# Conformer block: rows of whole chunks transposed by DMA instead of TensorE, with a new plan

## The chip, the cores and the metric

The kernel runs on one core of one Trainium2 chip. The core has five engines, each with its own in-order queue: TensorE (PE, matrix products and transposes into PSUM), VectorE (DVE), ScalarE (ACT), GpSimd (POOL) and SyncE (SP, which here only issues transfers). The metric is the device time of one execution, the median of several runs.

## The reference

One conformer block over x of shape (2, 4000, 144) in bfloat16: a half feed-forward, attention with 4 heads of 36, a gated depthwise convolution of 5 taps, a second half feed-forward, a last norm.

```python
h = _layernorm(x); h = _silu(h @ w_ff1a) @ w_ff1b; x = x + 0.5 * h
h = _layernorm(x); qkv = h @ w_qkv            # q, k, v: (B, 4, 4000, 36)
p = _softmax(einsum('bhqd,bhkd->bhqk', q, k) * 36 ** -0.5)
x = x + einsum('bhqk,bhkd->bhqd', p, v) @ w_o
h = _layernorm(x) @ w_pw1; a, b = h[..., :144], h[..., 144:]
h = a * _sigmoid(b); c = sum(pad(h)[:, i:i+4000, :] * dw[i] for i in range(5))
x = x + _silu(c) @ w_pw2
h = _layernorm(x); x = x + 0.5 * (_silu(h @ w_ff2a) @ w_ff2b)
return _layernorm(x)
```

## The kernel before, in words

**Tiling.** The 8000 tokens are 16 chunks of 500, 8 for each batch entry. A chunk is four blocks of 125 tokens; a block has its tokens on partitions in X and XN. Products need the features on partitions, 72 at a time in two halves, so every normalised row (here a "row" is one chunk's layer norm output or attention output) is turned over: into XT for the products of a feed-forward, of the attention's output and of the gate, into XTQ for queries, keys and values. That is five rows a chunk, 80 in all: the first feed-forward, queries/keys/values, attention output, gate, second feed-forward.

**How a row is turned.** `ln` (L888) takes the statistics on DVE and normalises block by block into XN, on POOL in the middle of the program, on DVE with POOL's power function in the front and the tail. `transp` (L877) then takes one PSUM bank, issues eight PE transposes (four blocks by two halves) and one copy out of PSUM, on DVE or, where ACT has less to do, on ACT (`flex`, L823). `parts` (L947) cuts a chunk into two half rows in the front (until the keys of the first batch entry, chunks 0 to 7, are done) and in the tail. Then a half row takes one bank, four transposes and one smaller copy. Chunk 0 goes by `pre_first` (L1139), the others by `ff1` and `pre2` (L1132, L1173), `post1` (attention output and gate, L1273) and `post2` (convolution and second feed-forward, L1398).

**Attention.** For each chunk of queries (a phase; the first two chunks have two phases each, L1515) the keys come in 62 tiles of 64 and a last one of 32. `emit_S` (L1541) computes the scores of a tile, four heads in two PSUM banks; `emit_exp` (L1555) has ACT take the exponential of both banks at once (128x1000) into a slot of PT; `emit_O` (L1623) multiplies PT with the values VA on PE. `dve_tile` (L1569) does a tile's exponential on DVE instead, in five steps: two int16 results from the score banks, taken one at a time, a mask (uint16), a product, a second mask. It yields two factors in two slots of PT, both of which are multiplied with the values. `due` (L1795) decides which tiles go there.

**Order.** A planner, which runs while the program is built, simulates the engines with costs written in the code and emits the operations in the order that it finds; POLICY holds its settings for 49 segments. `reorder` (L249) then shifts each engine's steps by the letters of ORDER (P is no shift; a letter for each step, trailing P's left off), and `place` (L227) gives each PSUM tile the bank that PLACES names, one digit for each tile in the order in which the tiles are taken. A pair of banks for ACT's exponential has one digit. So the order on every engine is fixed before the run, and an operation whose input is late stops its engine. Stores and loads are issued by SP, a few by ACT.

**Memory.** QT holds the queries of all 16 chunks. While the first two chunks' first phases wait for their second, their sums lie in SAVE, a part of QT not yet filled (L1466); `epilogue` (L1476) copies each chunk's result over queries that are used up.

Of the kernel before, what the change touches and what calls it, by code (L numbers as in the profile page):

```python
# [12 lines left out]
D = 144  # L13
# [23 lines left out]
        "PPPPPPPPPPPPQQRROKPPPPQQNQOQOPQOPPPPQOPRPNQOeOxRMMzPRKLHMNROMKMEOQLJOOQOIQKNQKMOOKOMOMNOOQNQQLQTNOYN"  # L37
        "NOSQTQKKTPQRSQWQ^BRW`EPWQ[GQ[EQ]RY]S?BBRWSZU?CCFUGQVTHKKNQSPPXPHQQNLOSNPQMPPPPPPQOPRRRMMPPPTPNPNQOSO"
        "PQMPPQOPPPPPPQOPQOQSNPRPLQOPPPPPPPPPPPPPPPPPPPPPPPPPPQOPPPPPQOPPQOPQOPPPPPPPPQOPPQOPPPQQNPPQOPPPRPRP"
        "RROIQOSQSQLLQOSOPNQQNSOOUPTLPVQUJQIWQKSQIMMTPPPLTPPROQSQHRMOQOPROOPPQOROOQQNPROOQQNQOPPTOOOOPPPPPPQQ"  # L40
        "NPPPPQQNPPQOPQQNPQOPPPQOPQOPQOQOPPPPPPPPPPPPPQOPQOPPPPPPPPPPPPPPPPPPPQSNPQRLOPPPPPPPPQOPQQNPPPPPQOPP"
        "PQQNPPPQTNOOQNPPPPPPPPPPPPPQRPMQOPPQOPPTOOPNQQNPROOSSNNNUPNSNOMQQQRLUNOOOOROOPROOPPPPQOPSPNQNQQQMPPS"
        "OOQNPPPRPNQOUPNOPNPPROOQQNQQQMPRPNQRNQNPQORPQMQOPQQNQOPPPQOPPPPPPPPPQOPQOPQQNPPPPPPPPPPQOPPPTOOOOSOP"
        "RPSKOOQTNOORNTPMORRMRRRKRLRRRLRRKRRRKSQKRRLTPLTOMRNQMQQSMSNROLQQSMOOQQNQQNQSNPRRLNROOQQNPQOQQQMSPNQQ"
        "MQQQRLQQQLQSNROULPNRNNQQQMROOQQQMRPNQQNQQNQQQMQRNQQRLQRMQQRLRPSLPRMSPMQRMSPMQRRLQRLQQMQRRTLPLTNOPRMQ"
        "QQTKPNQQTLPNQQRLQNQQRRRKTTKNNQMRPNPPPPQOQQNQOPROQNQOPQOQOQOPQQNPPPPPPPPPPPPPPPPPPPPPPPPPPROOPPPPQOPP"
        "PPPPROOPSOPNPPPPPPROOPPPPPPPPPPPPPPPPPPQOPPPPPPQOPQOPPQQNPPPPPPPPPQOPPPPPPPPPPPPPPPPQOPPSPNRPRPQQIPP"
        "WOOOOQRMQRKOQOQWNOQNNRNNROQNQOPQQNPPPQOPPPPQOPPPROOPPPPPPPPPPPQOPPPPPPPPPPPPPQOPPPPPQOPPPQQNPPPPPPPP"
        "PPPROOPPRPNPPPPPPPPPPPPPTOQNNPPPQOPQOTUPMMNOQQSMOQNQTNOORNQSMOQSMSOMQQMRROMQSSSSKMKQQNPRPNROOPPPPQQN"
        "PQQNPQOPSPNOPPSOOOPPPPROOPPQOPPPPPPPPPPPPPPPPPPPPRSQSLLOPPQOPQOPQQNPPQOQOQOQOPPQOQOPQOPQOPPPPPPPPPPP"  # L50
        "QOPQOPPPPPPPQOPPPQOPPPPPQOPPPQOQOSQNQQLPPPPPPPPRORNOPPPPPPPQOPPPQOQQQQLROOQOQQQMQOQQQMQQQMQOQQQQLPPP"
        "PPPPPPPPPPPPPPQOPPQOQOPRPNPPPPPQRNVNOQNNQNRPNQQSMOQNRPQMRPNSOOQNQOPPPSOOTNOOOPQOQQQQLPQOQQNROOQQNQOQ"
        "QQQQKQQQMPPRPQQQKQQNROQNPPPPPPPPPPPQQNQOPPPQQNSPNOPPSPRRLMPQOPPQOPQOPPPQOQOROOSOOSNOQNQOQQQMPPROOPPP"
        "PPQQNPPSOOOPPPPPPPPPPSOOOPPPROOQQRMQNPQOPPPPQQNPPPPPPPPPPPPQOPPQOPPSOOOPQOTQNNOPQOPPQOQQNPPPPPUPNYNY"
        "MMNVNUOPSHIIPQOPPPQQNPQOPPUOQNNQQQLPPPPPPPPPPPQQSPLOQOPRPNPQOTOPNOQOPPROQRMOPQOSOPQMROOQQNPPPRPNPQOP"
        "PPPPPPPPPPPPPPPPPPPPPPPQQNPPQOPPPPQOPPPPPPPPPPPPPPPPTPPPQQQITUSMMMMQOQOQQNRRSSLLNQOPROOPPPPQOROOPPQQ"
        "QQQKPPQQQQLPPPPPPPPPPPPPPPPPPPPPPPPPPPPPPPPPPQQNSQNTRLNQMPPQOPPQOQOPPPPSSPSQKKQOQQQMQQQMQQQMQRNOQOPQ"
        "RNOSPNQQQLQQQMQOQQNPQQNPPPQQQQLRVNNOOOOPRSNNQQMQQQMTOOOOPPPPSQNNQOPPQOPRPNPPTRNNNPRPNQOPPQOPPSOOOPPP"
        "PPPPPQOPQOPQQNPSSNNNPQQNPQRNQQMQOQQNROOPPQQQQLPQSNOQNQRNOSORNNQOPQOQOPQOPPQRPMQTTMNNNSOOQNPPQOQOPPPQ"
        "OPROOPQOPPPPPPPPPPPPPPPPPPPPSOPNQOPPRPNQOPPQOPQQNQQNRPNPQQNQOQQQMROOQOPRRSMRLRMQQMQOSPPRLOPQOPQQNPPP"  # L60
        "QOPPPPPPPPPPPPPPPPPRRNNPPPPRPNRPRMRNOPPQQNROOPQQNPPPPPPPPRPNQQNROOPQSNOQNPRRNSPLQNPQOPPQOPPQOPPPQOQQ"
        "NPPPQQNPPPPPPPPPPQOPPPPPPPPPPPPPPQOPQOQOQOQOPPPPPPPPQOPPPPPPQOQOQOPPQOROOQQQQLQQNQRRMQMROOPQQNQRPMQO"
        "ZQOXLNNWMPXKKOUIOLNNQSNPNQQNROOPVOOOOOOQOROQQMQRPMQOPPQOPPPPPQOPPPPPPQOPPPPQOPQOSOPQMROOPPPPQOPPPPPP"
        "PPPPPPPPUOQNNRSMNSNROMPPQOPPPPPPPPPPPQOPQOQOQOPPQOQRRMRMOQRRRLTPKRNNQQQMPSOOOPQQNPSOOOPPPQOPPRPNVPUM"
        "QSLRRRIRRGNPQOZOPX_WKLPKKKKQQQSPGUIOOPNPQOROOPPPQOPSQOMPPPPPPPPPPPPROOPPPROOPQOPPPPQO"
    ),
    "act": (
        "PPPPPPPPPPPPROOPQQNPPPPPPPPPPPPPQRSMNOPPPQOQQNQOQQSMPSMOOPPQOQOPPPPPPPPPPPPPPPPPPQRNOPROOPPPPPPPPPQO"
        "PPPPPPPPPPPPPPPPPPPPPPPPPPPPPPPPPPPPPPPPPPPPPPPPPPPPPPPPQOQQNQQNPPPPQOPPPPPPPPPPPPPPPPPPQOPPPPPPPPPP"
        "PPPPPPPPPPPPPPPPPPPPPPPPPPPPPPPPPPPPPPPPPPQOPPPPPPPQOPPQOPPPPPPPPPPPPPQQNPQOPPPPPPPPPPPPPPPPPPPPPPPP"  # L70
        "PPPPPPPPPPQQNPPPPPPPPPPPPPPPPPPPPPPPPPPPPPPPPPPPPPPPPPPQOPPROOPPPPPROOQOPPPPPPPPPPPPPPPPPPPPPPPPPPPP"
        "PPPPPPPPPPPPPPPPPPPPPPPPPPPPPPPPPPPPQOPPPPPPPPPPPPPPPPPPPPPPPPPPPPPPPPPPPPPPPPPPPPPPPROOPPQRNOPPPPPP"
        "PPPPPPPPPPPPPPPPPPPPPPPPPPPPPPPPPPPPPPPPPPPPPPPPPPQOPPPPQOPPPPQOPPPPPPPPPPPPPPPQOPPPPPPPPPPPPPPPPPPP"
        "PPPQOPPPPPQOPPPQOPPQOPPPPPPPPPPPPPPPPPPPPPPPPPPPPPPPPPPPPPPPPQOPPPPPPPPPPPPPPPQOPPPROOROOPPPQOPPPPPP"
        "PPPPPPPPPPPPPPPPPPPPPPPPPPPPPPPPPPPPPPPPPPQQNPPPPPPPPPPQOPPPPPPPPPPPPPPPPPPPPPPPPPPPPQOPPPQOPPPPPPPP"
        "QOPPPPPPPPPPPPPPPPPPPPPROOPPPPPPPPPPPPPPPPPPPPPPPPPPPPPPPPPPPPPPPPQOPPPPPPQOPPPPPPPPPPPPPPPPPPPPPPPP"
        "PQOPQOPPPPPPPPPPQOPPPPPPPPPPPPPPPPPPPPPPPPPPPPPPPPPPPPPPPPPPPPPPPPPPPQOPQOPPQOPPQOPPPQOPPPQOPPPPPPPP"
        "PPPPPPPPPPPPPPPPPPPPPPQOPPPPPPPPPPPPPQOPQOPPPPPPPPPPPPPPPPSSNNNQQNROOPPPPPQQNPPPQRPQQQQIPQOPPQO"
    ),
# [1812 lines left out]
```

## Time and profile before

| | us |
|---|---|
| median of 3 runs | 905.8 (905.73 to 905.96) |
| span of the profiled execution | 903.7 |
| first / last exponential on ACT starts | 19.7 / 869.5 |
| exponentials on ACT, on DVE | 841, 167 |
| TensorE's granted clock, mean | 0.997 |

Line 353 is the helper that records every operation, so groups are told apart by the tiles that they write and read (out<-in). "DVE COPY XT<-PS" is the copy after a row's transposes, "PE MATMUL PS<-IDENT,XN" the transposes themselves, "PT<-PS" the exponentials. Behind a group stand its busy time, the mean of one in ns, and the engine's idle time ahead of it with the releaser.

### The profile page before, as it was taken

What the parts mean: (1) busy time and instruction counts of PE and PEld (TensorE: products, weight loads), DVE (VectorE), ACT (ScalarE), POOL (GpSimd) and SP (SyncE); (2) the same over time, 40 slices, a digit from 0 to 9 for tenths busy, and PEclk for the clock granted to TensorE, in tenths of its full rate; (3) what the DMA queues carried; (4) which work ended last, traced back from release to release, by engine and by line L of the source; (5) the groups of instructions that cost most, each with busy time, mean ns of one, the idle gap of its engine ahead of it and who ended that gap; (6) DMA issues with size and microseconds to landing.
All of it is one profiled execution on the core that took longest, in us unless ns stands there. A gap on an engine that the chain in (4) does not pass through costs nothing.

```text
span 903.7 us, 27474 instructions
## 1 busy us (share of the span) xinstructions
PE 878.2 (97%) x11946; PEld 409.1 (45%) x11946; DVE 808.1 (89%) x1756; ACT 869.2 (96%) x1105; POOL 278.5 (31%) x519
## 2 busy tenths in 40 slices
PE   8999999999999999999999999999999999999996
PEld 6644434454443443444444444444434444434366
DVE  8988888889999998999988799897899799978987
ACT  6899999999999999999999999999999999999984
POOL 5121213136211702421404441270215460323143
PEclk9999999999999999999999999999999999999998
DMA  4000000000000000000000000000000000000000
GB/s 123 27 2 2 1 2 1 2 3 1 2 3 1 3 2 3 1 3 1 2 2 1 15 2 2 15 8 1 1 3 8 14 9 2 3 1 10 6 8 27
DMA packets 7322, 7.36 MB, mean 8 GB/s; under 512 B 2376, under 2 KB 7202, under 8 KB 7202
## 3 DMA queue, kind: packets, MB, share of 16 engines
q1 hardware_dynamic: 5786, 5.00, 1.8%
q8 instruction: 93, 1.52, 0.7%
q10 hardware_dynamic: 1416, 0.62, 0.3%
q14 instruction: 27, 0.22, 0.1%
HBM read 3.31 MB, written 2.30 MB: 6 GB/s over the span
## 4 chain that ended last, share of the span: by engine, by line
ACT 48%; PE 42%; DVE 6%; POOL 2%; issue 1%; DMA 0%; POOLq 0%; DVEq 0%
ACT PT L353 43%; PE PS L353 42%; ACT TH L353 5%; DVE PT L353 3%; POOL RS L353 1%; POOL XN L353 1%; DVE ST L353 1%; DVE HT L353 1%; DMA X<-in_x_dram 0%; DVE QT L353 0%; DVE XN L353 0%; DVE XT L353 0%; DVE KT L353 0%; DVE X L353 0%; DVE RS L353 0%
## 5 line engine op out<-in xcount | busy, mean ns | idle before, releaser
L353 ACT ACTIVATE PT<-PS 128x1000 bf16<-128x1000 f32 (+1 forms) x841 | 777.7, 1063 | 5.9 <-PE PS L353 4.0
L353 PE MATMUL PS<-QT,KT 64*64 64x500 bf16 x3968 | 416.1, 385 | 10.7 <-ACT PT L353 6.0
L353 PE MATMUL PS<-PT,VA 64*37 64x500 bf16 x4636 | 394.6, 373 | 2.1 <-DVE PT L353 0.9
L353 DVE TENSOR_SCALAR PT<-PS 128x500 int16<-128x500 f32 x334 | 222.1, 670 | 21.0 <-PE PS L353 18.5
L353 PEld LDWEIGHTS PS<-QT,KT 64*64 64x64 bf16 x3968 | 122.2, 104 | 216.1 <-ACT PT L353 122.3
L353 POOL TENSOR_SCALAR RS<-ST 125x4 f32<-125x4 f32 x112 | 34.0, 304 | 475.2 <-DVE ST L353 469.5
L353 PEld LDWEIGHTS PS<-PT,VA 64*37 64x37 bf16 x4636 | 131.9, 96 | 95.9 <-DVE PT L353 22.0
L353 DVE TENSOR_SCALAR PT<-PT 128x1000 uint16<-128x1000 uint16 x334 | 137.7, 421 | 2.6
L353 POOL TENSOR_SCALAR XN<-X,RS 125x144 bf16<-125x144 bf16 x224 | 132.4, 605 | 8.0 <-DMA out_dram<-XN 2.3
L353 POOL TENSOR_TENSOR RS<-RS,NHALF 125x4 f32<-125x4 f32 (+1 forms) x101 | 95.3, 948 | 94.7 <-DVE RS L353 89.9
L353 DVE TENSOR_TENSOR PT<-PT 128x1000 bf16<-128x1000 bf16 x167 | 113.5, 682 | 1.6
L353 ACT ACTIVATE TH<-PS 128x500 bf16<-128x500 f32 (+3 forms) x198 | 107.0, 563 | 3.3 <-PE PS L353 2.1
L353 DVE SCALAR_TENSOR_TENSOR HT<-TH,PS 128x500 bf16<-128x500 bf16 (+1 forms) x135 | 81.1, 616 | 18.8 <-ACT TH L353 18.4
L353 PE MATMUL PS<-XT,WA 72*128 72x500 bf16 (+2 forms) x280 | 71.6, 359 | 0.5 <-DVE XT L353 0.3
L353 DVE SCALAR_TENSOR_TENSOR X<-PS,X 125x288 bf16<-125x288 f32 x128 | 57.2, 451 | 12.4 <-PE PS L353 10.9
L353 DVE BATCH_NORM_STATS2 ST<-X 125x6 f32<-125x288 bf16 (+1 forms) x160 | 66.1, 447 | 1.2 <-DMA X<-in_x_dram 0.8
L353 PE MATMUL PS<-WB,HT 128*125 128x144 bf16 (+1 forms) x640 | 52.4, 230 | 0.0
L353 PEld LDWEIGHTS PS<-WB,HT 128*125 128x125 bf16 (+1 forms) x640 | 44.3, 136 | 13.0 <-issue 5.1
L353 PE MATMUL PS<-IDENT,XN 125*72 125x125 bf16 x512 | 42.9, 221 | 3.1 <-POOL XN L353 1.7
L353 DVE COPY XT<-PS 72x1000 bf16<-72x1000 bf16 (+2 forms) x65 | 40.1, 617 | 4.7 <-PE PS L353 4.2
L353 PEld LDWEIGHTS PS<-IDENT,XN 125*72 125x72 bf16 x512 | 31.8, 112 | 23.4 <-issue 11.4
L353 PEld LDWEIGHTS PS<-XT,WA 72*128 72x128 bf16 x280 | 20.3, 97 | 30.4 <-issue 7.1
(86 smaller groups left out, 573.3 us busy)
## 6 DMA issues: line engine op xcount, KB each, us to landing
X<-in_x_dram SPq DMA_DIRECT2D x16, 140.6 KB
out_dram<-XN SPq DMA_DIRECT2D x14, 140.6 KB
WA<-in_w_ff1a_dram ACTq DMA_DIRECT2D x1, 144.0 KB
WB<-in_w_ff1b_dram ACTq DMA_DIRECT2D x1, 144.0 KB, 2.8
WA<-in_w_ff2a_dram SPq DMA_DIRECT2D x1, 144.0 KB
WB<-in_w_ff2b_dram SPq DMA_DIRECT2D x1, 144.0 KB
out_dram<-XN SPq DMA_DIRECT2D x2, 70.3 KB
WQKV<-in_w_qkv_dram ACTq DMA_DIRECT2D x1, 121.5 KB
```

What stands on the lines that cost most here:

```text
L353: ins = getattr(eng, o.name)(*o.a, **o.k)
```

## The change

- XN, AN and XT get blocks of 128 columns for each half of 72 (`[NB, 2, 128]`), so that a row is 128 x 1024; XT's buffer XTB can be read as before or as DMA leaves it, with a block every 256 columns. The columns between are cleared once for each buffer by POOL, ten clearings. A stored row uses XN densely, as XNC.
- `small(c)` says where half rows remain: in the tail, and in the front for chunks 0 to 3 alone (FULL = 4). Before, the whole front had them. Chunks 4 to 7 are therefore normalised as whole rows on POOL.
- A whole row is turned by one `dma_start_transpose` from SP. For queries, keys and values the result goes to an XT buffer, and two more transfers copy it into XTQ. There is no PSUM bank, no PE transpose and no copy by DVE or ACT for such a row.
- QT shrinks to a ring of NQR = 12 chunks. The queries of chunks 12 to 15 wait until the attention of chunks 1 to 4 has left its slot. SAVE moves to the second batch entry's keys.
- POLICY, ORDER and PLACES are new throughout. Their lengths:

| table | before | after |
|---|---|---|
| PLACES, digits | 1778 | 1735 |
| ORDER pe, act, dve, pool, sp, letters | 2885, 1095, 1613, 127, 13 | 2885, 1075, 1646, 135, 94 |

```diff
+    NQR = 12
+    NLANE = 12
+    FULL = 4
+    LAT_C = 2.2
+    SP_T = 1.2
+    LAT_T = 2.5
-    XN = sb("XN", [NXN, NB, D])
+    XN = sb("XN", [NXN, NB, 2, 128])
-    XT = sb("XT", [NXT, 2, CW])
+    XTB = sb("XTB", [NXT, 2 * NB * 128])
-    QT = sb("QT", [2, N])
+    QT = sb("QT", [2, NQR * CH])
-    AN = sb("AN", [NAN, NB, D])
+    AN = sb("AN", [NAN, NB, 2, 128])
...
+    XT = XTB[:, :, 0:2 * CW].rearrange("p s (k n) -> p s k n", k=2)
+    XTD = XTB[:, :, :].rearrange("p s (i k n) -> p s i k n", i=NB, k=2)
+    def xt(s, k, i0, i1):
+        if s in by_dma:
+            return XTD[0:HD, s, i0:i1, k, 0:TB]
+        return XT[0:HD, s, k, i0 * TB:i1 * TB].rearrange("p (i n) -> p i n", i=i1 - i0)
...
+    def small(c):
+        return mode["tail"] or mode["front"] and c < FULL
...
+    def dma_transp(src, rk, s, wk):
+        j = lanes[0] % NLANE
+        lanes[0] += 1
+        yield need("sp")
+        by_dma.add(s)
+        op("sp", "dma_start_transpose", XTB[:, s, :].rearrange("p (j n) -> p j n", n=128),
+           src.rearrange("p i k n -> p (i k n)"), q=f"t{j}", r=[rk], w=wk + [("LANE", j)], cost=SP_T, lat=LAT_T)
...
-        calm = mode["front"] or mode["tail"]
+        calm = small(c)
+        if n == NB and not calm and not store and ("XN", u) not in clear:
+            clear.add(("XN", u))
+            yield need("pool")
+            op("pool", "memset", XN[:, u, :, :, :], 0.0, w=[("XN", u)], cost=0.8)
...
     def ln_tr(c, s, bs, e=False):
         u = yield from ln(c, bs, e)
         rows, c0 = TB + e, bs[0] * TB
+        if len(bs) == NB and not small(c):
+            yield from dma_transp(XN[:, u, :, :, :], ("XN", u), s, [("XT", s, i) for i in bs])
+            xnp.give(u)
+            return
...
     def ln_trq(c, bs):
...
+        if len(bs) == NB and not small(c):
+            s = yield need("sp", xtp)
+            yield from dma_transp(XN[:, u, :, :, :], ("XN", u), s, [("XT", s, i) for i in bs])
+            xnp.give(u)
+            yield need("sp")
+            for k in range(2):
+                j = lanes[0] % NLANE
+                lanes[0] += 1
+                op("sp", "dma_start", XTQ[0:HD, k, c0:c0 + CH].rearrange("p (i n) -> p i n", i=NB),
+                   XTD[0:HD, s, :, k, 0:TB], q=f"t{j}", r=[("XT", s, i) for i in bs],
+                   w=[("XTQ", c % CPB, i) for i in bs] + [("LANE", j)], cost=0.6, lat=LAT_C)
+            xtp.give(s)
+            return
...
-    def parts():
-        return [range(0, 2), range(2, 4)] if mode["front"] or mode["tail"] else [range(0, 4)]
+    def parts(c):
+        return [range(0, 2), range(2, 4)] if small(c) else [range(0, 4)]
...
+        wrap = nm == "WQ" and c >= NQR
+        bk = yield need("pe", banks, dur=0.42, cond=(lambda: not saved) if over or late else (
+            lambda: c - NQR + 1 in otf_done) if wrap else None)
...
         def part(bs):
-            yield from transp(AN[0:TB, a, bs[0]:bs[-1] + 1, :], ("AN", a),
-                              XT[0:HD, s1, :, bs[0] * TB:(bs[-1] + 1) * TB], [("XT", s1, i) for i in bs], len(bs))
+            if len(bs) == NB and not small(c):
+                yield from dma_transp(AN[:, a, :, :, :], ("AN", a), s1, [("XT", s1, i) for i in bs])
+            else:
+                by_dma.discard(s1)
...
-    SAVE = QT[:, 1, T:T + 4 * CH * NQ].bitcast(F32).rearrange("p (c k n) -> p c k n", c=NQ, k=2)
+    SAVE = KT[:, 1, 1, 0:4 * CH * NQ].bitcast(F32).rearrange("p (c k n) -> p c k n", c=NQ, k=2)
```

The products read XT through `xt` and `xt1` (one block), and `blocks` gives their PSUM side the same shape. `lat` is what the planner takes for the time from the end of an operation to its result.

More of the change, by code (lines that the diff above doesn't have):

```diff
@@ L126 @@
+    '36321430641340365200542643146141321'
 )
@@ L227, in place @@
     def place(self, slot, n):
-        no, at = len(self.tiles), int(PLACES[len(self.tiles)])
+        no, at = len(self.tiles), slot if PLACES is None else int(PLACES[len(self.tiles)])
         self.tiles.append(tuple(range(at, at + n)))
@@ L809, in setup_qk @@
                    cost=0.3)
+    clear = set()
     def now(k):
@@ L881, in transp @@
             for i in range(n):
-                op("pe", "transpose", ps[:, k, i, 0:rows], src[:, i, k * HD:(k + 1) * HD], IDENT[0:rows, 0:rows],
+                op("pe", "transpose", ps[:, k, i, 0:rows], src[:, i, k, 0:HD], IDENT[0:rows, 0:rows],
                    r=[rk, "ID"], w=[("ps", bk)], cost=0.055, kind="f")
@@ L886, in transp, with halves, ln @@
         banks.give(bk)
-    def ln(c, bs, e=False):
+    def halves(ap):
+        return ap.rearrange("p (k d) -> p k d", k=2)
+    def ln(c, bs, e=False, store=False):
         n, b0, rows = len(bs), bs[0], TB + e
+        xn = (lambda u, j: XNC[0:rows, u, j, :]) if store else (lambda u, j: XN[0:rows, u, j, :, 0:HD])
+        xi = (lambda j: X[0:rows, c * NB + b0 + j, :]) if store else (lambda j: halves(X[0:rows, c * NB + b0 + j, :]))
         xe = ["XE"] * e
@@ L916, in ln @@
             for j in range(n):
-                op("act", "activation", XN[0:rows, u, j, :], X[0:rows, c * NB + b0 + j, :], ACT.Identity,
+                op("act", "activation", xn(u, j), xi(j), ACT.Identity,
                    bias=RS[0:rows, u, 2, j:j + 1], scale=RS[0:rows, u, 0, j:j + 1],
@@ L935, in ln_tr @@
         rows, c0 = TB + e, bs[0] * TB
-        yield from transp(XN[0:rows, u, 0:len(bs), :], ("XN", u), XT[0:HD, s, :, c0:c0 + len(bs) * rows],
+        if len(bs) == NB and not small(c):
+            yield from dma_transp(XN[:, u, :, :, :], ("XN", u), s, [("XT", s, i) for i in bs])
+            xnp.give(u)
+            return
+        by_dma.discard(s)
+        yield from transp(XN[0:rows, u, 0:len(bs), :, :], ("XN", u), XT[0:HD, s, :, c0:c0 + len(bs) * rows],
                           [("XT", s, i) for i in bs], len(bs), rows)
@@ L968, in mm2 @@
         for k in range(2):
-            op("pe", "matmul", PSV[0:rows, bk, 0:CH], lhsT=W0[0:HD, k, m0:m1], rhs=XT[0:HD, s, k, 0:CH], start=k == 0,
+            op("pe", "matmul", blocks(PSV[0:rows, bk, 0:CH]), lhsT=W0[0:HD, k, m0:m1], rhs=xt(s, k, 0, NB), start=k == 0,
                stop=k == 1, r=[("XT", s, i) for i in range(NB)] + wk, w=[("ps", bk)], cost=c_pe(CH), kind="f")
@@ L988, in ff_tile @@
                 for g in (1, 0):
-                    op("pe", "matmul", PSV[:, bk, 0:2 * TB], lhsT=WE[0:HD, k, 64 - 64 * g:192 - 64 * g],
-                       rhs=XT[0:HD, s, k, g * 2 * TB:(g + 1) * 2 * TB], start=k == 0 and g == 1, stop=k == 1 and g == 0,
+                    op("pe", "matmul", blocks(PSV[:, bk, 0:2 * TB]), lhsT=WE[0:HD, k, 64 - 64 * g:192 - 64 * g],
+                       rhs=xt(s, k, 2 * g, 2 * g + 2), start=k == 0 and g == 1, stop=k == 1 and g == 0,
                        r=[("XT", s, 2 * g), ("XT", s, 2 * g + 1)] + [(nm, "a", j) for j in (1, 2, 3)],
@@ L1067, in proj @@
         cc = c % CPB
-        over = nm == "WQ" and p == 1 and c >= CPB
-        late = nm == "WQ" and p == 0 and c >= NCH - 4
-        bk = yield need("pe", banks, dur=0.42, cond=(lambda: not saved) if over or late else None)
+        over = nm == "WK" and p == 1 and c >= CPB
+        late = nm == "WQ" and p == 0 and NQR - 4 <= c < NQR
+        wrap = nm == "WQ" and c >= NQR
+        bk = yield need("pe", banks, dur=0.42, cond=(lambda: not saved) if over or late else (
+            lambda: c - NQR + 1 in otf_done) if wrap else None)
         for k in range(2):
@@ L1076, in proj @@
         copy(dst, PSV[:, bk, 0:CH], [("ps", bk)], [(nm + "T", c)] + [("SAVE", i) for i in range(NQ) if over]
-             + ["OTF0"] * late, CH, scale=Q_SCALE if nm == "WQ" else 1.0)
+             + ["OTF0"] * late + [("WQT", c - NQR), ("OT", c - NQR), ("OT", c - NQR + 1)] * wrap, CH, scale=Q_SCALE if nm == "WQ" else 1.0)
         if nm == "WK" and cc == CPB - 1:
@@ L1133, in ff1 @@
         s = yield need("dve", xtp)
-        kids = S.spawn(ln_tr(c, s, bs) for bs in parts())
+        kids = S.spawn(ln_tr(c, s, bs) for bs in parts(c))
         yield need("pe", kids=kids)
@@ L1176, in pre2 @@
         yield need("dve")
-        kids = S.spawn(ln_trq(c, bs) for bs in parts())
+        kids = S.spawn(ln_trq(c, bs) for bs in parts(c))
         yield need("pe", kids=kids)
@@ L1292, in after @@
             yield from gen
-        kids = S.spawn(part(bs) for bs in parts())
+        kids = S.spawn(part(bs) for bs in parts(c))
         if c == NCH - 1:
@@ L1495, in epilogue @@
         else:
-            op("dve", "tensor_copy", OTF[:, :, :], ps, r=rk, w=["OTF", "OREL"], cost=c_dve(2 * CH))
+            op("dve", "tensor_copy", OTF[:, :, :], ps, r=rk, w=["OTF", "OREL"] + k0, cost=c_dve(2 * CH))
+        otf_done.add(c)
         a = yield need("dve", anp)
+        if ("AN", a) not in clear:
+            clear.add(("AN", a))
+            yield need("pool")
+            op("pool", "memset", AN[:, a, :, :, :], 0.0, w=[("AN", a)], cost=0.8)
         for zz in range(2):
@@ L1859, in bass_standalone__conformer_family_zipformer__speech_kernel @@
     R.stats = stats
-    R.reorder(ORDER)
+    if ORDER is not None:
+        R.reorder(ORDER)
     R.finish(group_qs=("w0", "w1", "w2", "w3"))
```

204 lines of the change are left out of this document (107 added, 97 removed), and 92 rows, old and new, of the table POLICY.

## The prediction

> **What bounds the kernel now.** I read the busy shares first, then the same by stages, then the groups of instructions, then the chain of waits.
>
> ```profile
> span 903.7 us, 27474 instructions
> PE 878.2 (97%) x11946; PEld 409.1 (45%) x11946; DVE 808.1 (89%) x1756; ACT 869.2 (96%) x1105; POOL 278.5 (31%) x519
> 0.00:20.00 20.00, 17.15 (x238) 15.02 (x239) 16.13 (x60) 11.02 (x23) 10.74 (x30) 1.00 0.46 122
> 20.00:850.00 830.00, 814.75 (x11118) 362.49 (x11118) 747.60 (x1569) 820.10 (x1021) 249.81 (x458) 1.00 0.02 5
> 850.00:904.00 54.00, 46.30 (x603) 31.60 (x591) 44.38 (x129) 38.12 (x63) 17.97 (x32) 0.95 0.05 15
> 200.00:300.00 100.00, 99.63 (x1390) 43.58 (x1386) 94.54 (x189) 97.89 (x119) 30.87 (x54) 1.00 0.01 2
> 500.00:600.00 100.00, 98.77 (x1338) 43.77 (x1330) 89.85 (x183) 99.72 (x126) 37.04 (x74) 1.00 0.03 8
> ```
>
> The columns of a stage are its length, then busy time of PE, PEld, DVE, ACT, POOL, the granted clock, the DMA share and GB/s. ACT idles 34.5 us in all: 9.0 before 20 us, 9.9 in the long middle stage, 15.6 after 850. So the middle stage, 830 of 903.7 us, is paced by ACT (98.8% busy). DVE is at 90.1% there, at best 94.5% in 100 us. PE shows 98%, but its ends are modelled and overlap, so I read PE from what it is given to do.
>
> ```profile
> ACT 48%; PE 42%; DVE 6%; POOL 2%; issue 1%; DMA 0%; POOLq 0%; DVEq 0%
> 853.05 23.25 PE PS L353 x296
> 876.34 17.58 PE PS L353 x223
> L353 ACT ACTIVATE PT<-PS 128x1000 bf16<-128x1000 f32 x825 | 769.5, 1071 | 5.8 <-PE PS L353 4.0
> L353 DVE TENSOR_SCALAR PT<-PS 128x500 int16<-128x500 f32 x334 | 222.1, 670 | 21.0 <-PE PS L353 18.5
> L353 DVE TENSOR_SCALAR PT<-PT 128x1000 uint16<-128x1000 uint16 x334 | 137.7, 421 | 2.6
> L353 DVE TENSOR_TENSOR PT<-PT 128x1000 bf16<-128x1000 bf16 x167 | 113.5, 682 | 1.6
> L353 PE MATMUL PS<-PT,VA 64*37 64x500 bf16 x4636 | 394.6, 373 | 2.1 <-DVE PT L353 0.9
> ```
>
> The chain alternates between ACT's exponentials and PE, and from 853 us to the end it is PE alone, the tail of the last chunks. A key tile's exponential costs ACT 769.5/825 = 0.933 us, or DVE (222.1+137.7+113.5)/167 = 2.834 us. 841 tiles go to ACT (16 of them halves), 167 to DVE: 1008 in all.
>
> **The tiles that change hands.** Time can only leave the middle stage if exponentials leave ACT. The number is in the diff: the bank table holds one digit for each PSUM tile, 1778 before, 1735 after, 43 fewer. A PE transpose of a row takes one bank. Whole-chunk rows by the copies' forms: 52 into XT (51 on DVE, 1 on ACT) and 8 into XTQ; chunks 4 to 7 have 16 half rows besides. All 76 tiles go. An exponential on ACT takes one entry, on DVE two. So 76 − 43 = **33 tiles go from ACT to DVE**, if nothing else changes its number of tiles. 12 rows each for the feed-forward and for queries, keys and values, 15 each for attention and gate, 14 for the second feed-forward make 68 DMA transposes.
>
> ```profile
> L353 DVE COPY XT<-PS 72x1000 bf16<-72x1000 bf16 x51 | 34.4, 674 | 3.6 <-PE PS L353 3.1
> L353 DVE COPY XTQ<-PS 72x1000 bf16<-72x1000 bf16 x8 | 5.4, 676 | 1.8 <-PE PS L353 1.6
> L353 DVE COPY XT<-PS 72x500 bf16<-72x500 bf16 x13 | 5.3, 411 | 1.2 <-PE PS L353 1.1
> L353 DVE TENSOR_SCALAR XN<-X,ST,RS 125x144 bf16<-125x144 bf16 x92 | 24.1, 309 | 1.2 <-POOL RS L353 1.0
> L353 DVE TENSOR_SCALAR RS<-ST 125x2 f32<-125x2 f32 x40 | 6.4, 161 | 0.4
> L353 PE MATMUL PS<-IDENT,XN 125*72 125x125 bf16 x508 | 42.5, 221 | 3.1 <-POOL XN L353 1.7 <-DVE XN L353 1.2
> ```
>
> *ACT.* 33 × 0.933 = 30.8 us less. If ACT alone still paced the stage with the idle time it has, the span would be 903.7 − 30.8 = 872.9.
>
> *PE.* 60 × 8 + 16 × 4 = 544 transposes go, at 42.5/508 = 0.084 us 45 us of shown busy time. A tile on DVE is multiplied with the values twice, four more matmuls of 394.6/4636 = 0.085: 33 × 4 × 0.085 = 11 us come. Net 34 us less, as much as ACT loses, so PE does not become the bound.
>
> *DVE.* Copies go: 34.4 + 5.4 + 16 × 0.411 = 46.4. The front chunks 4 to 7 get their normalised rows from POOL: 32 × 24.1/92 = 8.4 and 16 × 0.16 = 2.6 go. Together 57.4. Come: 33 × 2.834 = 93.5. **DVE has 36 us more than before.** Nearly all of it falls in the middle stage: 747.6 − 57.4 + 93.5 = 783.7 us of work. This is the term that decides. At the 94.5% that DVE held at best, 783.7 needs 829 us, and all that ACT gained is lost again; at ACT's 98.8% it needs 793, less than ACT's own 799. DVE's 94.5% was reached while ACT and PE paced, so it is no ceiling; yet its instructions have to wait for both. I take the middle, 96.7%: 783.7/0.967 = 810 us.
>
> *POOL.* The four front chunks' rows (32 of 0.605 us, with power and sums) and ten clearings are added, some 40 us on an engine that is 31% busy; bounds from nothing to that, taken as nothing.
>
> ```profile
> L353 POOL TENSOR_SCALAR XN<-X,RS 125x144 bf16<-125x144 bf16 x224 | 132.4, 605 | 8.0 <-DMA out_dram<-XN 2.3
> L353 POOL TENSOR_TENSOR RS<-RS,NHALF 125x4 f32<-125x4 f32 x59 | 65.9, 1117 | 6.6 <-DVE RS L353 2.0
> L353 POOL TENSOR_SCALAR RS<-ST 125x4 f32<-125x4 f32 x112 | 34.0, 304 | 475.2 <-DVE ST L353 469.5
> L353 POOL TENSOR_TENSOR RS<-RS,NHALF 125x2 f32<-125x2 f32 x40 | 28.1, 712 | 87.2 <-DVE RS L353 87.0
> L353 POOL MEMSET U<- 128x640 bf16 x1 | 0.6, 639 | 0.0
> L353 PE MATMUL PS<-U,DG 128*128 128x500 bf16 x15 | 5.8, 384 | 0.0
> L353 PE MATMUL PS<-XT,WA 72*128 72x500 bf16 x232 | 65.2, 378 | 0.5 <-DVE XT L353 0.3 <-DVE HT L353 0.2
> X<-X SPq DMA_DIRECT2D x1, 0.6 KB, 1.7
> X<-in_x_dram SPq DMA_DIRECT2D x16, 140.6 KB
> 0.72 4.17 DMA X<-in_x_dram
> 514.75 313.77 SPq L353 DMA_DIRECT2D out_dram<-XN  x10
> ```
>
> *Gapped operands.* XT filled by DMA has its four blocks of 125 at a step of 256, so matmuls read with gaps. The convolution reads U so already: 384 against 378 ns for a dense operand. Nothing.
>
> *The transfers.* No DMA transpose stands in this trace. Each moves 128 × 1024 × 2 B = 256 KB. From below: the small SBUF copy landed in 1.7 us. From above: the first load, 140.6 KB in 4.17 us, scaled by size, 7.6 us. The opening stage moved 122 GB/s: 1.7 + 2.15 = 3.85 us, which I take, nearest to it being the stage with many transfers. The planner reckons with 1.2 + 2.5 = 3.7. SP had ten stores in 314 us; 68 transposes at 3.85 and 24 copies of 72 KB at some 2 us are 310 us in 830. A transpose that waits on SP for POOL's row holds up the next transposes and the stores; PE's products wait for the former, nobody for the latter. At 3.85 the order that was drawn for 3.7 holds, ACT having two tiles of 0.93 us in store: cost taken as nothing, bounds in the third rival.
>
> The Trainium skill ("VectorE: DVE Perf Modes", The three transpose paths) speaks against the change: a 128x128 transpose is given as 390 ns on TensorE, 1309 by DMA. Eight blocks one behind the other would be 10.5 us, an estimate from that page. "DMA: Bandwidth & Descriptors" (Latency and other measured facts) gives DMA transposes 261 GB/s, which is 1.0 us for 256 KB and would leave 2.7 with the 1.7 us row. No run shown here has either.
>
> *Front.* Chunks 4 to 7 get their rows later.
>
> ```profile
> L353 ACT ACTIVATE PT<-PS x841: 573/1050/1330, 19.7 to 869.5; 128x1000 bf16<-128x1000 f32 x162, 128x500 bf16<-128x500 f32 x7
> ```
>
> A row takes 2 × 0.304 + 1.117 + 4 × 0.605 = 4.1 us on POOL against 0.161 + 0.712 + 2 × 0.262 = 1.4 for a half row, and the transfer 3.85 instead of a copy of 0.41: for two rows and the copies into XTQ 5.4 + 6.9 + 2 = 14 us for the first such chunk. Chunk 4's keys are wanted from tile 31 of the first pass, 31 × 0.933 = 29 us after the first exponential at 19.7, and the chunks run side by side, so that it can begin earlier. Taken as nothing; once 14 us without that cover.
>
> *The ring of queries.* Queries of chunks 12 to 15 wait for the attention of chunks 1 to 4, done in the first third of the phases; chunk 12's are wanted after three quarters. Nothing.
>
> **Sum.** 903.7 − 830 + 810 = 883.7 us of span. The median lies 905.8 − 903.7 = 2.1 above the span of the profiled execution: **886 us**. What is late next is DVE, with ACT at (820.1 − 30.8)/810 = 97%.
>
> **Rivals.**
> 1. *DVE becomes the bound and gives the gain back.* At 94.5%: 783.7/0.945 = 829, span 903, time 905. For it: 21.0 us of idle ahead of its first pass over the scores, waiting for PE. Against: PE, on which it waited there, has 34 us less to do. From 95.5% down to this it is 897 to 905.
> 2. *ACT alone paces.* 872.9 + 2.1 = 875, down to 868 if its own 9.9 idle us shrink. For it: with PE relieved of 34 us, DVE gets its scores earlier. Against: DVE would have to be over 98% busy for 800 us.
> 3. *Late transposes: slower.* The order on PE is fixed, so a product whose row has not landed stops PE, and with it scores for ACT. ACT covers two tiles, 1.87 us; the plan covers 3.7. From a landing of 5.57 us on, each of 68 rows costs what is above: 886 + 68 × (L − 5.57). It eats the whole gain at L = 5.86, gives 922 at 6.1, and 1024 at the upper bound of 7.6. For it: 4.17 us for a load of half the size. Against: that was the first of the program, with weights beside it. By the Trainium skill's 1309 ns it would be certain: 886 + 68 × (10.5 − 5.57) = 1221.
> 4. *The change relieves PE alone:* the 43 entries come from other tiles, ACT keeps its 841 and the time stays at 904 to 906. Against: shifts of the DVE table grow from 1613 to 1646 although 76 copies go, which needs some 30 tiles of five steps.
>
> **Chances.** Forecast 0.50 (874 to 897 by DVE at 98% to 95.5%), first rival 0.17, second 0.10, third 0.18, fourth 0.05. About 0.2% (904.0 to 907.6) is what a measurement of this kernel can tell from no change. Faster: 0.50 + 0.10 + 0.11 of the first = 0.71; same 0.04 + 0.05 = 0.09; slower 0.18 + 0.02 = 0.20. The range 868 to 912 leaves out 0.03 below and 0.13 of the third rival.
>
> **What will show it.** Steps right: ACT's exponentials near 808 and DVE's int16 instructions near 400; 96 PE transposes left; DVE near 844 us of 884; transposes landing in 3 to 5 us; hardly any wait of PE for a DMA. Wrong, if DVE's share in the middle stays under 95%, if PE's weight loads wait for XT or XTQ from DMA by more than 30 us in all, or if the exponentials on ACT are still over 830.

## The result, and the profile after

| | before | after | ratio, 95% interval |
|---|---|---|---|
| first measurement, median us | 905.88 | 897.39 (893.85 to 898.36) | 0.9899 (0.988 to 0.9918) |
| second measurement of the same kernel | 905.54 | 894.16 (893.88 to 894.32) | 0.9875 (0.986 to 0.989) |
| span of the profiled execution (first) | 903.7 | 892.0 | |

The kernel is faster, by 8.5 and 11.4 us, where 20 were forecast. The four times of the first measurement go with the mean granted clock of TensorE in each (893.85 at 1.000, 896.57 at 0.997, 898.21 and 898.36 at 0.996); in the second, at 0.998 to 1.000, all lie within 0.5 us, and the kernel before keeps to 904.9 to 906.2 at 0.997 to 0.999, so what made the first spread isn't shown. The spans are compared below, at a clock of 1.000 after and 0.997 before; the second trace of the changed kernel has 892.4 at 0.998.

First the head of the page after: the span and the busy times.

```profile
span 892.0 us, 27205 instructions
PE 863.8 (97%) x11731; PEld 395.8 (44%) x11731; DVE 815.7 (91%) x1786; ACT 847.6 (95%) x1084; POOL 277.6 (31%) x543
ACT PT L353 53%; PE PS L353 33%; ACT TH L353 5%; DVE PT L353 4%; DMA XTB<-XN 1%; DMA X<-in_x_dram 0%; DVE ST L353 0%; DVE HT L353 0%; DVE X L353 0%; DVE KT L353 0%; DVE XN L353 0%; POOL RS L353 0%; ACT L353 0%; DVE QT L353 0%; DVE AN L353 0%
```

ACT has 21.6 us less to do, DVE 7.6 more. In the chain (third line) ACT's exponentials hold 53% and the transposes' landings 1%. Next the exponentials on ACT after (number; shortest, median and longest in ns; first and last start), the stage up to the last one with the stage behind it, and the stage behind the last one of before:

```profile
L353 ACT ACTIVATE PT<-PS x815: 581/1052/1338, 19.9 to 837.2; 128x1000 bf16<-128x1000 f32 x156, 128x500 bf16<-128x500 f32 x7
20.00:838.30 818.30, 798.36 (x10838) 336.52 (x10836) 755.49 (x1580) 810.24 (x1004) 247.35 (x486) 1.00 0.15 28
838.30:892.00 53.70, 48.31 (x658) 44.24 (x656) 43.91 (x148) 26.18 (x59) 16.84 (x26) 1.00 0.07 21
```

```profile
870.60:903.70 33.10, 25.85 (x313) 21.85 (x309) 27.11 (x92) 18.07 (x37) 11.26 (x16) 0.92 0.08 23
```

This is the account of the whole change. **The last exponential starts 32.3 us earlier (869.5 to 837.2), and the tail behind it is 20.6 us longer (33.1 to 53.7)**: −32.3 + 20.6 = −11.7, the difference of the spans. Not all of the 32.3 us is gained: the exponentials take 24.7 us less of ACT, but 8.1 us more of ACT's other work stand behind the last one (18.07 to 26.18 in the stages above), work that was put off and not saved. Up to the last exponential ACT is 99.0% busy (810.24 of 818.30), DVE 92.3%: ACT still paces. What is left over for the tail shows in one group, the additions to X, eight for each chunk (four places, two blocks at a time): those that start behind the last exponential, before and then after.

```profile
L353 DVE SCALAR_TENSOR_TENSOR X<-PS,X 125x288 bf16<-125x288 f32 (+1 forms) x16 | 7.0, 451 | 0.4
```

```profile
L353 DVE SCALAR_TENSOR_TENSOR X<-PS,X 125x288 bf16<-125x288 f32 (+1 forms) x26 | 11.5, 450 | 4.3 <-PE PS L353 4.2
```

16 additions were left before, 26 after: the exponentials got ahead of the chunks' own work by two and a half chunks' back halves (convolution and second feed-forward, four additions each). A second group grew there too: the fillers, products of the identity with itself that the planner puts on PE where it expects PE to pause. Their results are used by nothing, but PE's queue is in order, so what stands behind them comes after them. In the same two stages, before and then after:

```profile
L353 PE MATMUL PS<-IDENT 128*128 128x128 bf16 x37 | 3.4, 219 | 0.0
```

```profile
L353 PE MATMUL PS<-IDENT 128*128 128x128 bf16 x222 | 15.2, 219 | 0.0
```

And the rows, the tiles and the transfers after:

```profile
L353 DVE TENSOR_SCALAR PT<-PS 128x500 int16<-128x500 f32 x386 | 255.3, 670 | 19.8 <-PE PS L353 17.4
L353 DVE TENSOR_SCALAR PT<-PT 128x1000 uint16<-128x1000 uint16 x386 | 154.1, 414 | 1.6
L353 DVE TENSOR_TENSOR PT<-PT 128x1000 bf16<-128x1000 bf16 x193 | 129.7, 676 | 1.5
L353 PE MATMUL PS<-IDENT,XN 125*72 125x125 bf16 x108 | 10.2, 221 | 1.9 <-DVE XN L353 1.6 <-DVE HT L353 0.2
...
XTQ<-XTB SPq DMA_DIRECT2D x24, 70.3 KB
...
XTB<-XN SPq DMA_TRANSPOSE x50, 3.2
XTB<-AN SPq DMA_TRANSPOSE x15, 3.3
```

193 tiles are on DVE now instead of 167, so 26 changed hands. 65 rows go by DMA and land in 3.2 us. That is the middle of the seven landings that the view knows; by the semaphore times in the trace it is 3.1 for all 65, from 3.0 to 4.9 but for two of 6.5 and 6.7. The one of 6.5 is the 1% of the chain.

### The profile page after: what moved, and what is told of

The parts are those of the page before. It is cut to its first block, busy times and chain, and to the rows that moved or that the text cites. A ratio compares the mean times of both kernels' runs of the same rounds, so it can differ in the third digit from the quotient of the medians.

```text
span 892.0 us, 27205 instructions
## 1 busy us (share of the span) xinstructions
PE 863.8 (97%) x11731; PEld 395.8 (44%) x11731; DVE 815.7 (91%) x1786; ACT 847.6 (95%) x1084; POOL 277.6 (31%) x543
## 4 chain that ended last, share of the span: by engine, by line
ACT 59%; PE 33%; DVE 6%; DMA 1%; issue 0%; POOL 0%; SPq 0%; POOLq 0%; DVEq 0%
ACT PT L353 53%; PE PS L353 33%; ACT TH L353 5%; DVE PT L353 4%; DMA XTB<-XN 1%; DMA X<-in_x_dram 0%; DVE ST L353 0%; DVE HT L353 0%; DVE X L353 0%; DVE KT L353 0%; DVE XN L353 0%; POOL RS L353 0%; ACT L353 0%; DVE QT L353 0%; DVE AN L353 0%
## 5 line engine op out<-in xcount | busy, mean ns | idle before, releaser
L353 ACT ACTIVATE PT<-PS 128x1000 bf16<-128x1000 f32 x815 | 753.0, 1066 | 2.9 <-PE PS L353 1.3
L353 PE MATMUL PS<-PT,VA 64*37 64x500 bf16 x4740 | 417.7, 373 | 2.2 <-DVE QT L353 1.0
L353 DVE TENSOR_SCALAR PT<-PS 128x500 int16<-128x500 f32 x386 | 255.3, 670 | 19.8 <-PE PS L353 17.4
L353 POOL TENSOR_SCALAR RS<-ST 125x4 f32<-125x4 f32 x118 | 30.8, 261 | 473.7 <-DVE ST L353 467.9
L353 POOL TENSOR_TENSOR RS<-RS,NHALF 125x4 f32<-125x4 f32 (+2 forms) x97 | 92.1, 952 | 53.0 <-DVE RS L353 48.1
L353 DVE SCALAR_TENSOR_TENSOR HT<-TH,PS 128x500 bf16<-128x500 bf16 (+1 forms) x130 | 79.1, 614 | 10.2 <-ACT TH L353 9.3
L353 PE MATMUL PS<-XTB,WA 72*128 72x500 bf16 (+2 forms) x296 | 73.2, 350 | 2.3 <-DMA XTB<-XN 1.0
L353 DVE SCALAR_TENSOR_TENSOR X<-PS,X 125x288 bf16<-125x288 f32 (+1 forms) x128 | 57.2, 451 | 14.3 <-PE PS L353 13.3
L353 DVE BATCH_NORM_STATS2 ST<-X 125x6 f32<-125x288 bf16 x160 | 66.1, 448 | 1.1 <-DMA X<-in_x_dram 0.7
L353 PEld LDWEIGHTS PS<-XTB,WA 72*128 72x128 bf16 x296 | 21.2, 97 | 32.1 <-issue 10.9
L353 PE MATMUL PS<-U,DG 128*128 128x250 bf16 (+6 forms) x204 | 29.8, 264 | 0.1
L353 PE MATMUL PS<-IDENT 128*128 128x128 bf16 x341 | 24.2, 226 | 1.5 <-POOL NHALF L353 1.5
```

The costliest lines, as they stand in the source:

```text
L353: ins = getattr(eng, o.name)(*o.a, **o.k)
```

## Experiments

**1. Is it the transfers?** Three kernels: the same again; one that leaves the transfers out; one that makes every row's arrival late.

> The changed kernel as it is, for a second trace and as the base of the runs beside it. If the spread of its times (893.9 to 898.4 us) comes from transfers that land late now and then, this trace shows more waiting for XTB than 3 us, and its span is then some 4 us longer; if the spread has another cause, the waits for XTB stay at 3 us and the time goes elsewhere. Expected 894 to 898 us.

Measured 894.16, span 892.4, and PE with its weight loads waits 3.1 us in all for transposes. At this time late landings cost next to nothing. None of its four times is as high as 896 to 898, so whether the higher times of the first measurement came from late landings stays open.

`rows_stay` leaves out, after the order is fixed, every DMA transpose but the first into each buffer, and the copies into XTQ of chunks 8 to 15; the products read what the buffer holds.

```diff
+    seen = set()
...
+        R.tag = ("row", s) if s in seen else None
+        seen.add(s)
         op("sp", "dma_start_transpose", XTB[:, s, :]...
...
+            R.tag = ("copy", c) if c >= CPB else None
...
     if ORDER is not None:
         R.reorder(ORDER)
+    R.leave_out(lambda o: o.tag is not None)
```

> The changed kernel with all DMA transposes left out but the first into each XT buffer, and the copies into XTQ from chunk 8 on left out; the products wait only for the norm and read what lies in the buffers. Theory: transfers that land in 3.2 us are covered, so the time moves by less than 3 us. Rival: the chain of waits has 1% on XTB (some 9 us) and the rest hides in the order; then it gets 5 to 12 us faster.

Measured 893.75, ratio to before 0.9879 (0.9862 to 0.9895); 0.4 us under the change, which is nothing. The transfers cost nothing that shows in this order.

`rows_twice` issues each transpose twice; the products wait for the second.

```diff
         op("sp", "dma_start_transpose", XTB[:, s, :]..., q=f"t{j}", r=[rk], w=wk + [("LANE", j)], ...)
...
+        op("sp", "dma_start_transpose", XTB[:, s, :]..., q=f"t{j}", r=[rk], w=wk + [("LANE", j)], ...)
```

> The changed kernel with each row transposed twice, the products waiting for the second: every row lands some 1.2 us later and the transfers' load doubles. Theory that the transfers are covered with room: under 4 us slower. Rival, that they are just in time: 65 rows by up to 1.2 us, up to 78 us slower, by 20 us at least.

Measured 959.86, ratio 1.0621 (1.0578 to 1.0665). The second transpose goes to the same buffer, and SP waited for the first to land before it issued the second, so a row came some 3.3 us late and not by the 1.2 us of one more issue that was expected: by the semaphore times the second lands 6.4 us after the first was issued, the middle of 65 pairs. Its waits (us in all, times, longest) and its chain:

```profile
PEld PS L353 <- DMA XTB<-XN: 35.4, 19, 6.7
...
PE PS L353 <- DMA XTB<-XN: 28.1, 14, 6.2
...
SPq L353 <- DMA XTB<-XN: 114.8, 56, 3.9
...
SPq L353 <- DMA XTB<-AN: 33.8, 15, 4.0
...
PE PS L353 30%; ACT PT L353 24%; DMA XTB<-XN 14%; DVE PT L353 8%; POOL XN L353 3%; ACT TH L353 3%; DMA XTB<-AN 3%; POOL RS L353 3%; DMA XTQ<-XTB 2%; DVE ST L353 2%; DVE X L353 1%; SPq L353 1%; DVE KT L353 1%; DVE HT L353 0%; DVE QT L353 0%
```

SP stood 148.6 us at the first transposes (114.8 + 33.8), PE began to wait, and 65.7 us were lost, a good 1.0 us for each of 65 rows. PE's granted clock was 0.970 in that trace against 0.998, and no run separates its share. So the order hides a landing of 3.2 us, and not one of 6.4 on every row: the mechanism of the third rival, at a landing that only two of the change's 65 rows have. (Its formula gives 68 × (6.4 − 5.57) = 56 us there.)

**2. Is it the tail?** Work of chunks 11 and 12 that falls into the tail is left out after the order is fixed: in `tail_two_less` the second feed-forward (norm, row, products, addition), in `back_half_out` all that follows the gate, their last norm and their stores too.

```diff
+            S.cur.tag = R.tag = ("ff2", c)
...
+    R.leave_out(lambda o: o.tag in [('ff2', 11), ('ff2', 12)])
```

> The changed kernel with the second feed-forward (its norm, row and products) of chunks 11 and 12 left out; every other instruction stands in the same order. Theory: the 20 us that were given back are the unfinished chunks, so with two of them gone the stretch behind the last exponential shrinks by 8 to 16 us, and the time to 880 to 889. Rival: that stretch is set by the chain of waits of chunks 13 to 15 alone; then it stays within 3 us.

> The changed kernel with the whole back half (convolution, its product, second feed-forward, last norm and store) of chunks 11 and 12 left out, everything else in the same order. That leaves behind the last exponential about the chunks that the kernel before had there. Theory: the longer tail is work that is limited by DVE, 44 us of it in 54; leaving out two chunks takes some 13 us of DVE out, the tail falls to 38 to 42 us and the time to 878 to 883. Rival: the chain of waits of chunks 13 to 15 sets the tail; then no more than the 4 us that the two feed-forwards alone gave.

Measured 889.92 (ratio 0.9838, 0.9817 to 0.9858) and 885.28 (0.9773, 0.9757 to 0.9789): 4.2 and 8.9 us under the change. The stage behind the last exponential, of the one and then of the other:

```profile
838.30:887.70 49.40, 41.06 (x554) 36.60 (x552) 37.53 (x124) 20.72 (x46) 14.08 (x22) 0.97 0.08 22
```

```profile
838.60:883.50 44.90, 37.98 (x514) 33.70 (x512) 32.12 (x104) 19.68 (x43) 11.32 (x18) 0.98 0.06 18
```

DVE's work there went from 43.9 to 37.5 and 32.1, the stage from 53.7 to 49.4 and 44.9: some 0.7 us for each us of DVE's work. The exponentials ended where they had. So the end hangs on the chunks' work in the tail. But both experiments gave less than expected (8 to 16 us, and a time of 878 to 883), and with two chunks' back halves gone the tail is still 12 us longer than before's 33.1. DVE is 72 to 82% busy in these tails, so its work alone doesn't set their length. PE is busier, 83 to 90%, and the fillers are part of it. Both runs keep 214 of the 222 fillers (14.2 us of PE in each tail). Where the chunks' work is out, fillers that used to fill a wait may hold up what follows. In the trace PE goes straight on, without a wait, behind 98 of the 222 fillers of the change and behind 182 of the 214 in `back_half_out`. At 0.056 us from one to the next that is up to 5.5 and 10.2 us. No run leaves the fillers out, so how much of the tail is theirs, and how much is the chunks' work and its chains from product to addition to norm, is not shown.

**3. What is the operations' doing, and what the order's?** Both kernels with the planner's own order and banks, ORDER and PLACES unused:

```diff
+    global ORDER, PLACES
+    ORDER = PLACES = None
     R = Rec(nc)
```

> The kernel before with its shifts and its table of banks left away, in the planner's own order. 905 to 930 us; what it loses against 905.5 is what its shifts were worth.

> The changed kernel with the shifts of the order and the table of banks left away, so that every engine runs in the planner's own order. If the plan carries the change, it is 895 to 905 us and stays below the kernel before in its planner's order by 3 us or more. If the new shifts carry it, it is 905 to 930 us and no faster than the kernel before treated alike.

Measured 915.01 before and 912.37 after: 2.6 us apart. The tables take 9.2 us off the one (915.01 to 905.8) and 18.2 off the other (912.37 to 894.2). Their exponentials, before and then after:

```profile
L353 ACT ACTIVATE PT<-PS x841: 587/1038/1294, 21.0 to 878.2; 128x1000 bf16<-128x1000 f32 x163, 128x500 bf16<-128x500 f32 x6
```

```profile
L353 ACT ACTIVATE PT<-PS x815: 582/1038/1305, 20.7 to 853.5; 128x1000 bf16<-128x1000 f32 x156, 128x500 bf16<-128x500 f32 x7
```

24.7 us earlier, as much as 26 tiles are worth on ACT (26 × 0.933 = 24.3), and nearly all of it given back behind them: the spans are 913.5 and 911.4. The tail is where the operations' gain goes even without the tables: there too 26 additions stand behind the last exponential instead of 15, and 222 fillers instead of 37. The change was expected at 895 to 905 us if the plan carried it; 912.37 misses that, and what shows in the time comes mostly with the tables.

`before_rows_out` asks what the relief of PE and DVE is worth with no tile moved: in the kernel before, the eight PE transposes and the copy of each whole row whose buffer has been filled once are left out, the order kept.

```diff
+        gone = n == NB and all(w[0:2] in seen for w in wk)
+        R.tag = "row" if gone else None
...
+    R.leave_out(lambda o: o.tag == "row")
```

> The kernel before with the PE transposes and the copies of whole rows left out wherever the buffer was written before (most of the 60 rows), its order and its 841 exponentials on ACT kept; products read what lies in the buffers. Theory that ACT paces the middle: taking 35 us off DVE and some 40 off PE gives 2 to 8 us, no more than ACT's 9.9 us of idle time there. Rival, that DVE or PE paced: 15 us or more.

```profile
span 900.4 us, 26517 instructions
PE 855.4 (95%) x11506; PEld 383.8 (43%) x11506; DVE 781.2 (87%) x1702; ACT 866.7 (96%) x1104; POOL 272.0 (30%) x519
```

Measured 902.37, 3.4 us under before (ratio 0.9962, 0.9947 to 0.9977), with DVE at 27 us and PE at 23 us less work. By busy time that is less relief than the 35 and some 40 us expected. ACT paces, so the relief alone is worth little; the tiles that it lets move are what counts.

**4. Nearly the same operations in an order that keeps the chunks' work up.** `searched_further` is the changed kernel with other planner settings, and with the order on each engine and the banks searched for them; the source differs in nothing else. The search moves single steps and banks and replays the engines with the planner's costs; for the kernels before and after, that replay ended 12.8 us under the measured span. POLICY, TJ and FJ (lists of settings) have other values, and these:

```diff
-            shift = [ALPHABET.index(c) - 45 for c in table[e]]
+            shift = list(table[e])
...
-    FLEX = 0.3
+    FLEX = 0.25
...
-    ALONE = 3
+    ALONE = 4
...
-    BEND = 2.0
+    BEND = 1.4
-    ENDS = 1.6
+    ENDS = 1.5
...
-    TFIRST = 0.15
+    TFIRST = 0.25
```

> The changed kernel with other planner settings and with order and banks searched anew for them; the operations are the same in kind (the exponentials stay split as they are, within one or two). A replay of the engines with the costs written in the code puts the end 12 to 15 us under the measured span for the four kernels tried so far (890.9 against 903.7 for before, 879.4 against 892.2 for the change). For this kernel it gives 868.9, with the last exponential ending at 830.9 instead of 825.9 and a tail of 38.0 instead of 53.6. Theory (what the change lost it lost in the tail, because the chunks' work fell behind the exponentials; where it keeps up, the time follows): span 868.9 + 12.8 = 881.7, time 883.5, 881 to 887; last exponential on ACT starting near 842, tail near 40. Rival (the tail is set by the chains of the last chunks and an order can't shorten it; a later last exponential makes it later still): tail again 50 us or more behind a last exponential at 842, time 894 or above.

```profile
span 884.7 us, 26851 instructions
PE 853.8 (97%) x11538; PEld 385.3 (44%) x11538; DVE 809.9 (92%) x1760; ACT 846.4 (96%) x1082; POOL 289.0 (33%) x563
...
L269 ACT ACTIVATE PT<-PS x816: 587/1060/1290, 20.3 to 843.7; 128x1000 bf16<-128x1000 f32 x156, 128x500 bf16<-128x500 f32 x8
...
844.80:884.70 39.90, 33.10 (x395) 27.69 (x393) 32.82 (x106) 22.73 (x49) 16.57 (x30) 0.96 0.13 34
...
L269 DVE SCALAR_TENSOR_TENSOR X<-PS,X 125x288 bf16<-125x288 f32 (+1 forms) x18 | 7.7, 448 | 0.4 <-PE PS L269 0.3
L269 PE MATMUL PS<-IDENT 128*128 128x128 bf16 x65 | 5.3, 219 | 0.0
```

Measured **886.47** (886.14 to 886.74), ratio 0.9784 (0.977 to 0.9797); it beats both kernels. Its last exponential starts 6.5 us later than in the change (843.7), and its end is 7.3 us earlier: 18 additions and 65 fillers are left behind it instead of 26 and 222, and the tail is 39.9 us instead of 53.7. ACT has the work that it has in the change (846.4 us), DVE 5.8 us less (809.9): 192 tiles are on DVE, and 67 rows go by DMA, two more, since fewer are cut into halves. So another plan and order can shorten the tail, and the rival, by which an order cannot, is out.

`before_searched` gives the kernel before the same search, from its own tables and settings.

> The kernel before with its own planner settings, order and banks searched further, by the same search as in searched_further and for as long; the operations are those of before, rows turned by TensorE. The search from the tables of before ends at 886.9 in the replay of the engines (before itself 890.9), a search from the planner's own order, as searched_further began, at 887.3. Theory (with order searched alike the change itself is worth what ACT and PE are relieved of, and the little gain of the change as it stands is its order): span 886.9 + 12.8 = 899.7, time 901.6, 900 to 904, so that the change at an order searched alike gains some 15 us. Rival (it is the search that gains, not the change: the kernel before had as much left in its order): 890 or less.

```profile
span 901.8 us, 27510 instructions
...
L269 ACT ACTIVATE PT<-PS x841: 580/1060/1294, 19.8 to 867.2; 128x1000 bf16<-128x1000 f32 x164, 128x500 bf16<-128x500 f32 x5
```

Measured 903.56 (903.32 to 903.88), ratio 0.9979 (0.997 to 0.9988). The search finds 1.9 us in the kernel before, and 7.7 in the change together with its new settings. So searched, the two are 17.1 us apart, both in time (903.56 − 886.47) and in span (901.8 − 884.7): the last exponential 23.5 us earlier, the tail 6.4 longer (39.9 against 33.5; a last exponential takes 1.1, so that tail is 901.8 − 867.2 − 1.1). The two were not treated wholly alike: the planner's settings were changed for the change alone, and what other settings would give the kernel before is untested.

## Why the prediction was right in sign and too large

It had the sign, and the kernel as changed is at 894 to 897, not at 886. That `searched_further` comes to 886.47 does not bear the forecast out: there the last exponential starts at 843.7 and not at 849.5, the tail is 39.9 us and not 33.1, and the two nearly cancel.

- **The step that failed is the sum, 903.7 − 830 + 810.** It shortened the middle, by a pace of DVE, and kept the 54 us behind it as they were, a tail of 33.1 us behind the last exponential, without giving a reason. The runs show otherwise on both sides. By the sum the last exponential would have started at 869.5 − 20 = 849.5; it started at 837.2, so the middle came out 12 us shorter than forecast, and then 20.6 us came back in the tail. Work that was spread under the exponentials is not sped up with them: where ACT gets through its tiles sooner, the chunks' own work is left over, and plan and order decide how much. That this work makes the tail longer is shown by `tail_two_less` and `back_half_out`, 4.2 and 8.9 us of it; the share of the fillers that came with it stays open.
- **"DVE is the term that decides" was wrong.** It held 92.3% up to the last exponential, and 96.0% in 200 to 500 us (287.98 of 300, with ACT at 298.73), so the first rival's 94.5% was no limit. My 96.7% was never reached, for DVE got less work than the 783.7 us counted (755.49 up to the last exponential), and ACT paced. That is the second rival's mechanism. Its span of 872.9 is also close to what 838.3 and before's tail give, 838.3 + 33.1 = 871.4, but this is luck: its 30.8 us were to come from 33 tiles, and the 32.3 came from 26 tiles and from ACT's work put off. Like the forecast, it had the tail wrong.

```profile
200.00:500.00 300.00, 293.53 (x4106) 122.16 (x4104) 287.98 (x594) 298.73 (x363) 73.65 (x147) 1.00 0.15 25
```

- **33 tiles: mis-sized, 26.** The premise that nothing else changes its number of tiles failed for three chunks: 11, 12 and 13 have their second feed-forward in the tail now, as half rows. That makes 65 DMA rows instead of 68, and six half-row tiles that I had not counted: 76 − 6 − 43 = 27, and where the last one went isn't shown. At 0.933 us a tile the price was right: all exponentials on ACT, before and then after, fell by 24.7 us, against 26 × 0.933 = 24.3. ACT's other work grew by 3.1 us. With these the sum for ACT gives 903.7 − 24.7 + 3.1 = 882 us of span, an estimate for a tail that keeps its length; `searched_further` has 884.7.

```profile
L353 ACT ACTIVATE PT<-PS 128x1000 bf16<-128x1000 f32 (+1 forms) x841 | 777.7, 1063 | 5.9 <-PE PS L353 4.0
```

```profile
L353 ACT ACTIVATE PT<-PS 128x1000 bf16<-128x1000 f32 x815 | 753.0, 1066 | 2.9 <-PE PS L353 1.3
```

- **DVE +36: measured +7.6.** The part that comes was 93.5 for 33 tiles; the three groups of the tiles grew from 473.3 to 539.1 us, by 65.8. All else shrank by 58.2, against the 57.4 counted, but this agreement is luck: the copies fell by 42.4 (50.0 to 7.6) where 46.4 were counted, and the normalised rows by 3.4 (24.6 to 21.2) where 8.4 were.
- **PE −34: measured −14.4 by busy time.** The transposes and the products of the identity with itself that fill PE's pauses, before and then after:

```profile
L353 PE MATMUL PS<-IDENT,XN 125*72 125x125 bf16 x512 | 42.9, 221 | 3.1 <-POOL XN L353 1.7 <-DVE XN L353 1.2
...
L353 PE MATMUL PS<-IDENT 128*128 128x128 bf16 x156 | 12.5, 235 | 1.5 <-POOL NHALF L353 1.5
...
L353 PE MATMUL PS<-IDENT,AN 125*72 125x125 bf16 x128 | 10.2, 221 | 0.0
```

```profile
L353 PE MATMUL PS<-IDENT 128*128 128x128 bf16 x341 | 24.2, 226 | 1.5 <-POOL NHALF L353 1.5
...
L353 PE MATMUL PS<-IDENT,XN 125*72 125x125 bf16 (+1 forms) x112 | 10.4, 221 | 1.9 <-DVE XN L353 1.6 <-DVE HT L353 0.2
...
L353 PE MATMUL PS<-IDENT,AN 125*72 125x125 bf16 x8 | 0.6, 218 | 0.0
```

  The transposes went from 53.1 to 11.0, −42 against my −45. The fillers, which I had left out, came with the longer tail: +11.7, all of it behind the last exponential (15.2 − 3.4 = 11.8). The rest, for which I had +11, is +16.
- **Transfers at nothing: right.** 3.2 us in the middle against 3.85, two of 65 above the 5.57 from which the third rival counts a loss, 3 us of PE's waits in all, and `rows_stay` shows no gain without them. `rows_twice` shows how steep the other side is.
- **Front, ring and POOL at nothing: right as far as shown.** The first exponential starts at 19.9 against 19.7, POOL's busy time is 277.6 against 278.5, and POOL and SP have under 1% of the chain each. The front and the ring weren't tried alone.
- **The fourth rival** (PE relieved alone) is out, since 26 tiles moved; the nearest to its price is `before_rows_out`, which relieves PE and DVE with no tile moved: −3.4 us.
- Two small slips change nothing: by its own sum, 98% of DVE gives 875.5 us and not 874, and the chain before is PE's from 853 to 893.9 us, with POOL behind it, and not to the end.

What stays open: how the tail's length divides between the chunks' work, their chains and the fillers on PE. `searched_further` still has 6.4 us more of it than `before_searched`.

## What to carry to other kernels

When the engine that paces a stage is relieved, ask what other work ran under that stage: unless it moves up with it, it comes out behind, and the sum needs a term for the tail as well as for the stage. A kernel whose order is fixed by tables should be compared with its predecessor at an order searched alike: here the change with searched tables is worth some 17 us (its planner's settings were changed too), and its first tables showed 8 to 11 of it. Count moved tiles from every row that changes its form, those that grow too. And an experiment that leaves work out of a fixed order leaves the fillers around it in place, so it can show too little.

## What the runs showed of the hardware

- A DMA transpose of 128 x 1024 bfloat16 from SBUF to SBUF takes 3.1 us from issue to landing in the middle, by the semaphore times in the trace of the changed kernel (shortest 3.0, longest 6.7, 63 of 65 at most 4.9), and as much in `rows_twice` with 130 of them (3.0 to 7.4). The view's 3.2 is the middle of the seven that it knows. It keeps SP's queue for 1.23 us, where a plain store keeps it 0.35 and the copies into XTQ 0.81 (medians):

```profile
L353 SPq DMA_TRANSPOSE XTB<-XN x50: 1232/1234/2807, 23.3 to 830.0; - x50
L353 SPq DMA_DIRECT2D XTQ<-XTB x24: 796/812/997, 61.5 to 432.2; - x24
L353 SPq DMA_DIRECT2D out_dram<-XN x16: 254/351/480, 521.9 to 888.4; - x16
```

The Trainium skill's figure of 1309 ns for a 128x128 transpose by DMA ("VectorE: DVE Perf Modes", The three transpose paths), eight times over, had given 10.5 us as an estimate; the trace differs, 3.1 us for all eight, and decides.
